# Four experts tile by tile, finished rows on another queue, and weight loads moved and cut into 4 KB packets, in a retention layer with a mixture of experts behind it

## The chip, the cores and the metric

The kernel runs on one core of a Trainium2 chip. The metric is device time in microseconds (us); lower is better. A profile shows one execution: which engine ran which instruction when, what each waited for, and what every DMA queue moved. Four sessions on chips were used. The three of the experiments are named by the number of the chip: 9, 8 and 7 (the first session gave no number). Executions are marked fast or slow by their time and the clock granted to TensorE; verdicts use fast ones.

How much can be believed: the kernel before, submitted again unchanged, came out at a ratio of 1.0195 (95% interval 1.0095 to 1.0296) to itself on the same chip. The changed kernel gave 0.9535 on chip 8 and 0.9727 on chip 7. So here a difference of under some 2% between two kernels is not resolved by time alone, whatever its interval says, and the traces have to carry such arguments.

## The reference

```
# attention: per batch (4) and head (8), 768 steps, head size 64
state = gamma[h] * state + outer(k[t], v[t])
y[t]  = scale * q[t] @ state
# experts: x = y as 3072 rows of 512
do_compute = x @ w_skip > 0
e_idx = argmax(x @ w_gate); gate = softmax(...)[e_idx]      # 8 experts
out = x;  out[row] = x[row] + gate * (relu(x[row] @ w1[e]) @ w2[e])   # where do_compute
```

The weights w1 and w2 are 8 x 2 MB each in fp32. They are turned into bf16 while they are loaded, on GpSimd's queue.

## The kernel before

Attention is done in 16 units (4 batches x 4 pairs of heads), of 7 to 9 us each. A unit transposes q and k (`tps`), makes the scores (`atps`) and the chunk sums (`kvps`, which need v), applies them (`yps`), transposes the result into rows (`xall`, `xlast`) and stores the rows. Rows of three finished batches are routed while the last batch runs. Then come expert tasks: gather up to 256 rows of an expert as two tiles of 128, layer 1 (`hps`), layer 2 (`yps2`; the profile shows it as `yps` too), add (`yo`), scatter. "Tile by tile" experts have two tasks: the first tile, made of rows of the first three batches, can start before the last batch is routed.

```
def load(i):                      # q, k, v of unit i, on SyncE's queue
    for w, src, tag, bufs in ((kw, k, "kw", 2), (qw, q, "qw", 2), (vn, v, "vn", 4)):
        w[i] = poolQ.tile([128, 2 * G, R * D], FP32, tag=tag, bufs=bufs, name=tag)
        ...
        nc.sync.dma_start(out=w[i][:, :, :], in_=rows)          # 384 KB in rows of 512 B

def load_w(e, which, pl):         # GpSimd's queue, fp32 -> bf16
    w1b[e] = pl.tile([128, NDB, F], BF16, tag=f"w1_{e}", bufs=1, name="w1b")
    return G_.dma_start(out=w1b[e][:, :, :], in_=moe_w1[e].rearrange("(p a) f -> p a f", p=128))
    # 16 KB read in one piece per partition
    ...

def t_x(i, a):                    # rows of unit i
    ...
    for g in range(G):
        (A_ if last and g == 1 else nc.sync).dma_start(out=rows[...], in_=src[...])

wunits = (1, 4, 7, 9, 11, 12, 13, 13, 14, 15)   # units at which a weight load is issued
for i in range(NU):
    scale_qk(i + 1)               # GpSimd
    for _ in range(wunits.count(i)):
        load_w(*wjobs.pop(0), poolW)
    load(i + 3)
    ...                           # the unit; the first tiles are gathered in unit 15
NSPLIT = 3
tasks = [(e, [0]) for e in range(NSPLIT)] + [(e, [1]) for e in range(NSPLIT)] + [(e, [0, 1]) for e in range(NSPLIT, E)]
for t, (e, sts) in enumerate(tasks):
    hT = layer1(e, sts)
    ...                           # at t == 0: route the last batch, then gather the second tiles
    put_out(...)                  # VectorE adds, GpSimd scatters
    ...                           # gather later experts; six late weight loads, one a task
```

Of the kernel before, what the change touches and what calls it, by code (L numbers as in the profile page):

```python
# [18 lines left out]
def kernel(  # L19
# [17 lines left out]
    nc = tc.nc  # L37
    PE, V_, A_, G_ = nc.tensor, nc.vector, nc.scalar, nc.gpsimd
# [3 lines left out]
    E = moe_w1.shape[0]  # L42
# [7 lines left out]
    NU = B * NP  # L50
# [4 lines left out]
    CAP = 256  # L55
    NST = CAP // 128
    NEARLY = 10
    NSPLIT = 3
    scale = 1.0 / math.sqrt(D)
    lng = [math.log(1.0 - 2.0 ** (-5.0 - h)) for h in range(H)]  # L60

# [2 lines left out]
    poolW = ctx.enter_context(tc.tile_pool(name="wpool", bufs=1))  # L64
# [72 lines left out]
    for r in range(R):  # L137
        for hi in range(2):
            m = maskc[64 * hi : 64 * hi + 64, r, :, :]
            G_.affine_select(  # L140
                out=m, in_=m, pattern=[[1, R], [R, 64]], base=-r, channel_multiplier=-R, compare_op=ALU.is_ge, fill=0.0,
# [77 lines left out]

    w1b, w2b = {}, {}  # L220

    def load_w(e, which, pl):
        if which == 0:
            w1b[e] = pl.tile([128, NDB, F], BF16, tag=f"w1_{e}", bufs=1, name="w1b")
            return G_.dma_start(out=w1b[e][:, :, :], in_=moe_w1[e].rearrange("(p a) f -> p a f", p=128))
        else:
            w2b[e] = pl.tile([128, NFB, DM], BF16, tag=f"w2_{e}", bufs=1, name="w2b")
            return G_.dma_start(out=w2b[e][:, :, :], in_=moe_w2[e].rearrange("(p a) d -> p a d", p=128))


    QT, KT, ATm, Y, xT, xall = {}, {}, {}, {}, {}, {}
# [90 lines left out]
    def t_x(i, a):  # L322

        b, p = divmod(i, NP)
        last = i == NU - 1
        if p % 2 == 0 and a == 0:
            xall[b] = pool.tile([128, NS, 256], FP32, tag="xall", bufs=2, name="xall")
        if last and a == 0:
            xall["last"] = pool.tile([128, NS, 128], FP32, tag="xT", bufs=4, name="xlast")
        ps = ptile()  # L330
        for j in range(NT):
            PE.transpose(out=ps[:, j * 128 : (j + 1) * 128], in_=xT[i][:, a * NT + j, :], identity=ident[:, :])  # L332
        dst = xall["last"][:, :, :] if last else xall[b][:, :, p % 2 * 128 : (p % 2 + 1) * 128]
        A_.copy(
            out=dst[:, a * NT : (a + 1) * NT, :], in_=ps[:, :].rearrange("p (j t) -> p j t", j=NT),
        )
        rows = out[b * S : (b + 1) * S, :]
        if a == 0 or i < NU - 2 and p % 2 == 0:
            return
        src = xall["last"][:, :, :] if last else xall[b][:, :, 0:128] if i == NU - 2 else xall[b][:, :, :]  # L340
        cs = slice((p - 1) * 128 if i < NU - 2 else p * 128, (p + 1) * 128)
        for g in range(G):
            (A_ if last and g == 1 else nc.sync).dma_start(
                out=rows[g * 128 * R : (g + 1) * 128 * R, cs].rearrange("(p r) d -> p r d", r=R),
                in_=src[:, g * R : (g + 1) * R, :],
            )
# [160 lines left out]
    def gather(e, s_, first=True):  # L507
        n = (B - 1) * S if first and s_ == 0 else N
        ga = G_.indirect_dma_start(  # L509
            out=xgt[e, s_][:, :], out_offset=None, in_=out[0:n, :],  # L510
            in_offset=bass.IndirectOffsetOnAxis(ap=si[s_][:, e : e + 1], axis=0), bounds_check=n - 1, oob_is_err=False,
        )
        if first:
            no_dep(ga, scatters)
            gathers.append(ga)
# [15 lines left out]

    ALLV, IDS, GTS = slice(0, NV), slice(0, 2), slice(2, NV)
    wjobs = [(e, w) for e in range(E) for w in range(2)]
    wunits = (1, 4, 7, 9, 11, 12, 13, 13, 14, 15)
    routed = oh = None
    for i in range(NU):
        scale_qk(i + 1)
        if i == 1:
            parts = more_constants()
        for _ in range(wunits.count(i)):  # L540
            load_w(*wjobs.pop(0), poolW)
        load(i + 3)
        b, p = divmod(i - 2, NP)
        for a in range(2):
            t_qk(i, kw, KT, "KT", 1, a)
            t_qk(i, qw, QT, "QT", 2, a)
        if i >= 6 and p == 0:
            L = gate_rows(range(NP))
            routed = route(L)
        if i >= 6 and p == 2:  # L550
            tp = table(b - 1, oh, ALLV)
        s_at(i, 0)
        if i >= 6 and p == 2:
            add_table(tp)
        if i >= 2:
            t_x(i - 2, 0)
            t_x(i - 2, 1)
        if i >= 1:
            s_inter(i - 1)
        if i >= 2 and p == 3:  # L560
            gate_logits(b, range(NP))
        if i >= 6 and p == 0:
            cp = places(b - 1, routed[1])
            put_places(b - 1, routed[1], cp)
            oh = one_hots(b - 1, 0, G_)
            count(routed[1])
        if i == NU - 1:
            tp = table(b - 1, oh, ALLV)
            pad_counts()
            add_table(tp)  # L570
        s_at(i, 1)
        s_kv(i)
        if i >= 1:
            s_av(i - 1, 0)
            s_av(i - 1, 1)
        if i == NU - 1:
            s_av(i - 1, 2)
            slot_values(0)
            for e in range(NSPLIT):
                gather(e, 0)  # L580
        s_at(i, 2)
        if 1 <= i < NU - 1:
            s_av(i - 1, 2)
        if 1 <= i <= 3:
            parts[i - 1]()
        if i in (4, 5, 8, 9, 12, 13):
            n = (4, 5, 8, 9, 12, 13).index(i)
            V_.memset(xgt[n // 2, n % 2][:, :], 0.0)
        if i >= 6 and p == 0:
            gate_weight(b - 1, *routed, G_)  # L590
            put_rhs(b - 1, routed[1], ALLV, G_)
# [19 lines left out]
    poolE = ctx.enter_context(tc.tile_pool(name="esb", bufs=2, reuse_waits="tile"))  # L611
    for e, s_ in [(e, s_) for e in range(NSPLIT, E - 2) for s_ in range(NST)]:
        xgt[e, s_] = poolE.tile([128, DM], FP32, tag=f"xg{e}_{s_}", bufs=1, name="xgl")
    for n, (e, s_) in enumerate([(0, 0), (1, 0), (2, 0), (0, 1)]):
        xgt[E - 2 + n // 2, n % 2] = xgt[e, s_]
    poolX = ctx.enter_context(tc.tile_pool(name="wlate", bufs=1, reuse_waits="tile"))
    late = [(e, w, poolX) for e, w in wjobs]
# [45 lines left out]
    def clear_rows(e, s_):  # L663
        V_.memset(xgt[e, s_][:, :], 0.0)  # L664

    tasks = [(e, [0]) for e in range(NSPLIT)] + [(e, [1]) for e in range(NSPLIT)] + [(e, [0, 1]) for e in range(NSPLIT, E)]
    NAHEAD = 3
    after = None
    for t, (e, sts) in enumerate(tasks):
        hT = layer1(e, sts)  # L670
        if t == 2:
            tp = table(B - 1, oh, GTS, 1)
            V_.tensor_tensor(T[:, 1:2, GTS, :], T[:, 1:2, GTS, :], tp[:, :, :, :], ALU.add)
            V_.tensor_tensor(gt[1][:, :], T[:, 1, 2, :], T[:, 1, 3, :], ALU.add)
            V_.tensor_tensor(gt[1][:, :], gt[1][:, :], T[:, 1, 4, :], ALU.add)
        if t == 0:
            cp = places(B - 1, ha)
            put_places(B - 1, ha, cp)
            oh = one_hots(B - 1, 1)
            put_rhs(B - 1, ha, IDS)  # L680
        if t + 1 < len(tasks):
            e1, sts1 = tasks[t + 1]
            if 0 < t <= NAHEAD:
                for s_ in sts1:
                    x_cast(e1, s_)
            x_tr(e1, sts1)
            if NAHEAD <= t < len(tasks) - 2:
                for s_ in tasks[t + 2][1]:
                    x_cast(tasks[t + 2][0], s_)
        yps = [layer2(e, sts[0], hT, 0, t % 2)] if len(sts) == 1 else None  # L690
        if t == 0:
            prev = poolS.tile([128, E], FP32, tag="prev", bufs=1, name="prev")
            V_.tensor_tensor(prev[:, :], T[:, 1, 0, :], T[:, 1, 1, :], ALU.add)
            tp = table(B - 1, oh, IDS, 1)
            V_.tensor_tensor(prev[:, :], prev[:, :], tp[:, 0, 0, :], ALU.add)
            V_.tensor_tensor(si[1][:, :], prev[:, :], tp[:, 0, 1, :], ALU.add)
        if t == 1:
            for s_ in range(NST):
                clear_rows(NSPLIT + 1, s_)
                clear_rows(NSPLIT + 2, s_)  # L700
            count(ha)
            gate_weight(B - 1, Ls, ha)
            put_rhs(B - 1, ha, GTS)
        if t == 0:
            for n in range(NSPLIT):
                gather(n, 1)
            after = gathers[-1]
            for s_ in range(NST):
                clear_rows(NSPLIT, s_)
        with tc.issue_after(after.ins):  # L710
            for n, s_ in enumerate(sts):
                put_out(e, s_, yps[n] if yps else layer2(e, s_, hT, n, n))
        after = scatters[-1]
        with tc.issue_after(after.ins):
            for e1 in ((NSPLIT,), (NSPLIT + 1, NSPLIT + 2), (NSPLIT + 3,), (NSPLIT + 4,))[t] if t < 4 else ():
                for s_ in range(NST):
                    gather(e1, s_)
            if late:
                load_w(*late.pop(0))
# [63 lines left out]
```

## Time and profile before

| | before |
|---|---|
| timed runs, median of 3 | 245.79 us (244.05 to 247.15) |
| profiled run (the record marks it slow) | 237.03 us, span 235.0 us |
| TensorE busy | 199.5 us, 85% |
| first layer 1 starts | 157.28 us |
| last TensorE work | 223.6 us |

The page counts an engine's busy time; where the end is set is read from the chain of waits. The list of DMA issues tells how long each kind of transfer takes from issue to landing (count, KB each, median us). Two lines of it matter later:

```profile
vn<-in_v_dram SPq DMA_DIRECT2D x16, 384.0 KB, 7.3
out_dram<-xlast SPq DMA_DIRECT2D x2, 128.0 KB, 3.3
```

A v load usually lands 7.3 us after its issue, and the rows of the last unit in 3.3 us. The other lines are in the prediction below.

### The profile page before, as it was taken

What the parts mean: (1) busy time and instruction counts of PE and PEld (TensorE: products, weight loads), DVE (VectorE), ACT (ScalarE), POOL (GpSimd) and SP (SyncE); (2) the same over time, 40 slices, a digit from 0 to 9 for tenths busy, and PEclk for the clock granted to TensorE, in tenths of its full rate; (3) what the DMA queues carried; (4) which work ended last, traced back from release to release, by engine and by line L of the source; (5) the groups of instructions that cost most, each with busy time, mean ns of one, the idle gap of its engine ahead of it and who ended that gap; (6) DMA issues with size and microseconds to landing.
All of it is one profiled execution on the core that took longest, in us unless ns stands there. A gap on an engine that the chain in (4) does not pass through costs nothing.

```text
span 235.0 us, 8033 instructions
## 1 busy us (share of the span) xinstructions
PE 199.5 (85%) x3362; PEld 165.9 (71%) x3362; DVE 128.6 (55%) x432; ACT 79.4 (34%) x191; POOL 111.9 (48%) x131
## 2 busy tenths in 40 slices
PE   7779998999999999977998804988789999999900
PEld 7669987979899789966797604776557878866600
DVE  3557757649965488646298601458844644253120
ACT  2333354445543643452551400233203234322400
POOL 5169525324996356972177600503777754331220
PEclk9889999999999999999999965999979999999995
DMA  3899999999829999999999998260499999982120
GB/s 93 240 267 262 219 264 264 211 283 314 248 70 192 326 270 290 276 207 218 293 253 217 219 226 281 66 197 9 150 173 275 241 243 235 236 228 91 56 81 4
DMA packets 51096, 48.71 MB, mean 207 GB/s; under 512 B 3717, under 2 KB 47493, under 8 KB 49009
## 3 DMA queue, kind: packets, MB, share of 16 engines
q0 software_dynamic: 4864, 22.97, 43.3%
q1 hardware_dynamic: 45920, 25.06, 37.2%
q8 instruction: 28, 0.46, 0.8%
q10 hardware_dynamic: 272, 0.13, 0.2%
q14 instruction: 12, 0.09, 0.1%
HBM read 56.64 MB, written 10.49 MB: 286 GB/s over the span
## 4 chain that ended last, share of the span: by engine, by line
PE 70%; DMA 12%; DVE 7%; issue 3%; SPq 2%; POOL 1%; ACT 0%; DVEq 0%
DMA vn<-in_v_dram 12%; PE hps L630 11%; PE yps L640 11%; PE atps L257 10%; PE yps L308 8%; PE tps L243 8%; PE yps L297 7%; PE tps L332 5%; PE kvps L278 5%; PE gps L354 2%; SPq L92 2%; PE xtp L528 2%; DVE Zb L290 1%; DVE xgl L664 1%; PE lps L369 1%
## 5 line engine op out<-in xcount | busy, mean ns | idle before, releaser
L262 DVE TENSOR_TENSOR ATm<-atps,maskc 128x256 f32<-128x256 f32 x96 | 36.0, 416 | 31.7 <-PE atps L257 31.0
L290 DVE TENSOR_TENSOR Zb<-kvps,Zb 64x64 f32<-64x64 f32 x128 | 28.4, 222 | 17.1 <-ACT Zb L288 13.5
L113 POOL TENSOR_TENSOR ks<-kw,tk 128x768 f32<-128x768 f32 (+1 forms) x18 | 24.3, 1351 | 25.4 <-DMA kw<-in_k_dram 11.1
L257 PE MATMUL atps<-QT,KT 64*64 64x128 f32 x768 | 34.6, 284 | 1.4 <-DVE ATm L262 1.2
L634 ACT ACTIVATE hT<-hps 128x512 bf16<-128x512 f32 x32 | 19.1, 597 | 46.5 <-PE hps L630 46.5
L113 POOL TENSOR_TENSOR qs<-qw,tq 128x768 f32<-128x768 f32 x15 | 22.4, 1496 | 23.8 <-DMA qw<-in_q_dram 15.4
L308 PE MATMUL yps<-ATm,vn 64*64 64x128 f32 x768 | 31.1, 278 | 2.2 <-issue 2.2
L630 PEld LDWEIGHTS <-w1b 128*128 128x128 bf16 x352 | 30.6, 144 | 2.5 <-issue 0.8
L630 PE MATMUL hps<-xgT,w1b 128*128 128x128 bf16 (+1 forms) x352 | 31.1, 246 | 0.7 <-DVE xgT L529 0.7
L640 PE MATMUL yps<-w2b,hT 128*128 128x512 bf16 x128 | 30.7, 391 | 0.0
L257 PEld LDWEIGHTS atps<-QT,KT 64*64 64x64 f32 x768 | 24.0, 136 | 8.1 <-ACT QT L244 3.6
L651 POOL DMA_INDIRECT out_dram<-yo,si x16 | 16.3, 1021 | 23.9 <-DVE yo L648 15.9
L308 PEld LDWEIGHTS yps<-ATm,vn 64*64 64x64 f32 x768 | 24.8, 137 | 3.0 <-issue 2.9
L278 PE MATMUL kvps<-vn,ks 64*64 64x64 f32 x640 | 16.1, 230 | 10.0 <-DMA vn<-in_v_dram 10.0
L509 POOL DMA_INDIRECT xg<-out_dram,si x10 | 10.4, 1039 | 27.6 <-DVE gt L488 15.5
L278 PEld LDWEIGHTS kvps<-vn,ks 64*64 64x64 f32 x640 | 15.4, 145 | 10.4 <-issue 10.2
L640 PEld LDWEIGHTS <-hT 128*128 128x128 bf16 x128 | 12.5, 101 | 13.5 <-issue 1.6
L288 ACT COPY Zb<-kvps 64x64 f32<-64x64 f32 x32 | 6.6, 206 | 43.4 <-PE kvps L278 43.0
L297 PE MATMUL yps<-QT,Zb 128*128 128x128 f32 x160 | 20.7, 276 | 0.5 <-DVE xT L317 0.5
L297 PEld LDWEIGHTS yps<-QT,Zb 128*128 128x128 f32 x160 | 19.1, 192 | 0.9 <-ACT xT L317 0.7
L463 POOL TENSOR_SCALAR oh<-iotab,posT 128x256 bf16<-128x256 bf16 x18 | 16.3, 916 | 6.3 <-DVE posT L426 6.3
L243 PE MATMUL tps<-ident,ks 128*128 128x128 f32 x96 | 17.2, 287 | 1.7 <-ACT xT L317 1.3
(127 smaller groups left out, 261.3 us busy)
## 6 DMA issues: line engine op xcount, KB each, us to landing
w1b<-in_moe_w_dram POOLq DMA_DIRECT2D x8, 1024.0 KB, 11.0
w2b<-in_moe_w_dram POOLq DMA_DIRECT2D x8, 1024.0 KB, 10.9
vn<-in_v_dram SPq DMA_DIRECT2D x16, 384.0 KB, 7.3
kw<-in_k_dram SPq DMA_DIRECT2D x15, 384.0 KB, 6.2
qw<-in_q_dram SPq DMA_DIRECT2D x15, 384.0 KB, 6.8
out_dram<-xall SPq DMA_DIRECT2D x21, 256.0 KB, 6.3
kw<-in_k_dram SPq DMA_DIRECT2D x6, 64.0 KB, 1.9
qw<-in_q_dram SPq DMA_DIRECT2D x6, 64.0 KB, 1.9
```

Source lines behind the costliest of these rows:

```text
L113: eng.tensor_tensor(scaled[tag][:, ns, :, :], raw[:, ns, :, :], sc, ALU.mult)
L243: PE.transpose(out=ps[:, j * 128 : (j + 1) * 128], in_=in_, identity=ident[:, :])
L257: PE.matmul(out=ps[h][cp, j * C : (j + 1) * C], lhsT=KT[i][hp, s_, cp], rhs=QT[i][hp, R * g : R * g + R, cp], start=True, stop=True,)
L262: V_.tensor_tensor(out=ATm[i, n][:, h, :, :], in0=ps[h][:, :].rearrange("p (c t) -> p c t", c=2), in1=maskc[:, :, :, :].rearrange("p c r t ...
L278: PE.matmul(out=ps[c][64 * h : 64 * h + 64, g * D : (g + 1) * D], lhsT=kw[i][cp, R * g + r, h, :], rhs=vn[i][cp, h * G + g, r * D : (r + 1 ...
L290: V_.tensor_tensor(z, kv, Zb[i % 2][c - 1][hp, hp], ALU.add)
L297: PE.matmul(out=Y[i, c][:, g, :], lhsT=Zb[i % 2][ch - 1][:, :], rhs=QT[i][:, R * g : R * g + R, 64 * c : 64 * c + 64], start=(ch <= 2), st ...
L308: PE.matmul(out=Y[i, c][64 * h : 64 * h + 64, g, :], lhsT=vn[i][cp, h * G + g, r * D : (r + 1) * D], rhs=ATm[i, s_ // 2][cp, h, s_ % 2, :] ...
L463: eng.tensor_scalar(o[:, :], iotab[:, 128 * s0 :], posT[:, j : j + 1], None, ALU.is_equal)
L630: PE.matmul(out=ps[:, f, :], lhsT=w1b[e][:, db, f0 + f :: NFB], rhs=xgT[e][:, db, 0:n], start=(db == 0), stop=(db == NDB - 1),)
L634: A_.activation(out=hT[:, f0 : f0 + nf, 0:n], in_=ps[:, :, :], func=AF.Relu, bias=0.0, scale=1.0)
L640: PE.matmul(out=ps[:, :], lhsT=hT[:, fb, n * 128 : (n + 1) * 128], rhs=w2b[e][:, fb, :], start=(fb == 0), stop=(fb == NFB - 1),)
```

## The change

The intent: keep the DMA queue free for the last q, k and v, let rows and weights share it in shorter turns, and give TensorE one more task that doesn't depend on the last batch. Moving cuts only renumber lines.

```
-    NSPLIT = 3
+    NSPLIT = 4
...
-            return G_.dma_start(out=w1b[e][:, :, :], in_=moe_w1[e]...)
+            return G_.dma_start(out=w1b[e][:, :, :], in_=moe_w1[e]..., max_dma_last_dim=most)     # w2 likewise
...
-            (A_ if last and g == 1 else nc.sync).dma_start(
+            (nc.sync if i >= NU - 2 and (g != 1 or not last) else A_).dma_start(
...
-    wunits = (1, 4, 7, 9, 11, 12, 13, 13, 14, 15)
+    wunits = (1, 4, 7, 10, 12, 13, 14, 14, 15)
-            load_w(*wjobs.pop(0), poolW)
+            load_w(*wjobs.pop(0), poolW, 4096 if i >= 12 else None)
...
             for e in range(NSPLIT):
                 gather(e, 0)
+            load_w(*wjobs.pop(0), poolW, 4096)
...
-        if i in (4, 5, 8, 9, 12, 13):          # clears a gather tile
+        if i in (3, 4, 5, 8, 9, 12, 13, 14):
...
-    for n, (e, s_) in enumerate([(0, 0), (1, 0), (2, 0), (0, 1)]):     # tiles used again by the last two experts
+    for n, (e, s_) in enumerate([(0, 0), (1, 0), (2, 0), (3, 0)]):
-    NAHEAD = 3
+    NAHEAD = 4
-                clear_rows(NSPLIT + 2, s_)
-            for e1 in ((NSPLIT,), (NSPLIT + 1, NSPLIT + 2), (NSPLIT + 3,), (NSPLIT + 4,))[t] if t < 4 else ():
+            for e1 in (NSPLIT + t,) if NSPLIT + t < E else ():
```

I call the parts P (packets of 4 KB), W (where weight loads stand), R (rows on ACT's queue) and N (four experts tile by tile).

More of the change, by code (lines that the diff above doesn't have):

```diff
@@ L220, with load_w @@
     w1b, w2b = {}, {}
-    def load_w(e, which, pl):
+    def load_w(e, which, pl, most=None):
         if which == 0:
             w1b[e] = pl.tile([128, NDB, F], BF16, tag=f"w1_{e}", bufs=1, name="w1b")
-            return G_.dma_start(out=w1b[e][:, :, :], in_=moe_w1[e].rearrange("(p a) f -> p a f", p=128))
+            return G_.dma_start(out=w1b[e][:, :, :], in_=moe_w1[e].rearrange("(p a) f -> p a f", p=128), max_dma_last_dim=most)
         else:
             w2b[e] = pl.tile([128, NFB, DM], BF16, tag=f"w2_{e}", bufs=1, name="w2b")
-            return G_.dma_start(out=w2b[e][:, :, :], in_=moe_w2[e].rearrange("(p a) d -> p a d", p=128))
+            return G_.dma_start(out=w2b[e][:, :, :], in_=moe_w2[e].rearrange("(p a) d -> p a d", p=128), max_dma_last_dim=most)
     QT, KT, ATm, Y, xT, xall = {}, {}, {}, {}, {}, {}
@@ L585 @@
             parts[i - 1]()
-        if i in (4, 5, 8, 9, 12, 13):
-            n = (4, 5, 8, 9, 12, 13).index(i)
+        if i in (3, 4, 5, 8, 9, 12, 13, 14):
+            n = (3, 4, 5, 8, 9, 12, 13, 14).index(i)
             V_.memset(xgt[n // 2, n % 2][:, :], 0.0)
```

## The prediction

> **What bounds the kernel now.** I read the page first, then the chain that ended last, in order of time.
>
> ```profile
> span 235.0 us, 8033 instructions
> PE 199.5 (85%) x3362; PEld 165.9 (71%) x3362; DVE 128.6 (55%) x432; ACT 79.4 (34%) x191; POOL 111.9 (48%) x131
> DMA  3899999999829999999999998260499999982120
> PE 70%; DMA 12%; DVE 7%; issue 3%; SPq 2%; POOL 1%; ACT 0%; DVEq 0%
> ```
>
> TensorE is the bound (85% busy, 70% of the chain), but the DMA engines are full for most of the first 145 us, and one DMA carries 12% of the chain. The chain in order of time shows which (start, us, what):
>
> ```profile
> 116.24 0.60 PE atps L257 x16
> 116.89 27.14 DMA vn<-in_v_dram
> 144.16 1.44 PE kvps L278 x38
> ```
>
> This is the last v load, for unit 15, the last (batch, head pair). It took 27.14 us where the median v load takes 7.3 us. What TensorE really lost is in the waits:
>
> ```profile
> PE kvps L278 <- DMA vn<-in_v_dram: 10.0, 1, 10.0
> ```
>
> The windows view puts a size to the hole and its neighbours (us, busy PE, PEld, DVE, ACT, POOL, then clock, DMA share, GB/s):
>
> ```profile
> 117.00:134.00 17.00, 15.93 (x343) 14.03 (x334) 13.97 (x48) 6.82 (x19) 12.78 (x18) 1.00 1.04 236
> 134.00:144.20 10.20, 0.17 (x12) 0.07 (x5) 1.01 (x5) 0.00 (x0) 0.00 (x0) 0.64 1.01 242
> 144.20:157.30 13.10, 11.88 (x209) 10.21 (x210) 5.64 (x22) 4.02 (x10) 3.10 (x3) 0.89 0.59 172
> 157.30:175.00 17.70, 14.40 (x155) 10.34 (x155) 12.17 (x47) 3.71 (x7) 10.04 (x10) 0.90 0.42 97
> ```
>
> From 134.0 to 144.2 nothing computes while the DMA engines are full. Why the v load is late is seen in the DMA queues of the window 125 to 140 us:
>
> ```profile
> DMA packets 883, 3.33 MB, mean 222 GB/s; under 512 B 65, under 2 KB 517, under 8 KB 517
> q0 software_dynamic: 410, 2.97, 94.6%
> q1 hardware_dynamic: 469, 0.31, 8.4%
> ```
>
> 883 - 517 = 366 packets are weights (8 KB written, 16 KB of fp32 read), 517 - 65 = 452 are rows of 0.5 to 1 KB. The two queues take turns about packet for packet, and a weight packet lasts 0.946 x 15 x 16 / 366 = 0.62 us. A row waits for a weight packet each time.
>
> The SyncE timeline adds a second cause: the issue of finished rows stood 12.95 us in front of the loads of unit 15.
>
> ```profile
> 101.47 12.95 SPq L343 DMA_DIRECT2D out_dram<-xall  x3
> 114.52 1.09 SPq L87 DMA_DIRECT2D kw<-in_k_dram  x1
> 116.89 1.53 SPq L87 DMA_DIRECT2D vn<-in_v_dram  x1
> ```
>
> **What the Trainium skill says.** "DMA: Bandwidth & Descriptors", Queues, rings and completion order: each DMA engine goes round its queues packet by packet. The trace agrees (452 rows against 366 weight packets). Same page, SWDGE vs HWDGE vs iDMA: a packet should preferably be at most 4096 B, since the engine changes queue only at its end; these are 16 KB on the read side. Same page, Issuing engines are not separate DMA queues: another issuer gives no bandwidth, only issue time. That is the use made of ACT here; no row of before tests it under load. "TensorE: Matmul & The Clock Gate", Part 1: after some microseconds idle the clock falls to half until work has run again. The trace agrees: clock 0.64 in the hole, 0.89 after it, and `kvps x38` takes 1.44 us against 0.63 in earlier units.
>
> **The change part by part.**
>
> *4 KB packets from unit 12 on.* An estimate from the 0.62 us above: a quarter, 0.155 us. A v load is 384 KB in rows of 512 B, 768 packets, 48 an engine. Behind 16 KB packets: 48 x (0.62 + 0.03) = 31 us while weights last (0.03 us a row from the window 50 to 60: 5415 packets took 112.7% of 10 x 16 us). They were gone at about 144, so 27.1 us is the same thing. Behind 4 KB packets: 48 x (0.155 + 0.03) = 8.9 us. Total bytes don't change.
>
> *Fewer weights before the last loads.* Ten weight loads stay ahead of the experts, six late ones after. Jobs move from units 9, 11, 12, 13, 13, 14, 15 to 10, 12, 13, 14, 14, 15 and one after the first gathers. Two loads (117.88 and 118.45) that stood beside the last v load now come a unit later, after the last q has been scaled (about 123).
>
> *Rows out on ACT.* 21 of the 27 issues move. SyncE no longer waits for ACT's copies in program order, so the loads of unit 15 go out when their buffers are free. vn has four buffers, so v of unit 15 needs the end of unit 12, about 110. Issued at 110 and 9 us long, it lands by about 119 to 122, and it is wanted at 134. The wait of 10.0 us goes whole. ACT pays three issues of about 0.6 us (the one issue it has today took 0.67), 1.8 us every second unit; between the xall copies and the next Zb copy ACT idles 1.87 us in its timeline. So it is hidden, just. I charge 0.5 us in all.
>
> *Clock after the hole.* kvps 1.44 -> 0.65 us is 0.8 us on the chain; the slower yps, tps and gps after it add some 0.4. I take 1.2 us.
>
> *Four experts tile by tile.* One expert at 7.43 us (layer 1 3.53, transposes 0.45, layer 2 3.45) becomes two tasks of 3.9 us (174.95 to 178.87): + 0.37 us. What the fourth is to do is fill holes: tasks 0 to 2 last from 157.28 to 174.95, 17.67 us, against 3 x 3.9 = 11.7. But the chain there names DVE:
>
> ```profile
> 165.49 2.11 DVE L664 MEMSET xgl<- 128x512 f32 x4
> 169.34 0.31 DVE L438 TENSOR_TENSOR rhsT<-ha,vals 128x144 bf16<-128x144 bf16 x1
> 170.71 0.60 DVE L519 CAST xb<-xg 128x512 bf16<-128x512 f32 x1
> 171.98 2.97 PE yps L640 x8
> ```
>
> The gather for second tiles landed at about 166, so the 6 us are DVE's order, not a lack of rows. The change takes two of the four memsets (2 x 0.53 = 1.05 us) off this chain and puts two into units 3 and 14. TensorE also waits less, so `yps x8` may not fall to 2.97 us (1.73 elsewhere); I count 0.9 of those 1.24 us. Sum: - 1.05 - 0.9 + 0.37 = - 1.6 us.
>
> *GpSimd.* Four times the descriptors on six loads. A load of 128 packets takes 0.57 us to issue today; I expect 0.6 to 1.5. In unit 14 two of them stand before the one-hots, which now wait 1.7 us for VectorE; up to 0.5 us may reach TensorE.
>
> Sum on the span: 235.0 - 10.0 - 1.2 - 1.6 + 0.5 + 0.5 = 223.2 us, a factor of 0.950. The timed runs are longer than the profiled one (245.79 against 237.03); nothing here says why. The factor gives 233.4, the difference of 11.8 gives 234.0. A slower execution leaves the DMA queue, if anything, more room to hurt, so I go a little below: 233.
>
> **The rivals.**
>
> 1. *The wait moves.* DMA share is 0.99 to 1.04 from 70 to 134 us, so the queue as a whole may be the bound, and a load a unit later may starve unit 13 or 14. For: GpSimd already waited 7.7 us for a q load around 110 to 116. Against: TensorE lost nothing by that, and a weight load less lies ahead of the last loads. It would give back 3 to 8 us: 236 to 241.
> 2. *ACT becomes the stall.* SyncE's row issues took up to 11 us when the queue was full. If ACT's do as well, its KT and QT copies are late and TensorE stops with them, seven times. For: the waits under load. Against: ACT has a queue of its own, with at most three row issues in it. Two microseconds each would be 14 us: no gain, 246.
> 3. *The experts starve.* Late weights start after the first scatter, which now stands behind one more gather (1.3 us). The last weights landed at about 212 and were wanted at 220; the experts here end some 1.6 us earlier. Margin about 5 us; I see no loss, at most 2 us.
> 4. *A larger gain.* If the holes of tasks 0 to 2 do close with more work, up to 4 us more go: 229.
>
> **Range and chances.** Centre 233. Rival 1 in part or a few blocked ACT issues give the upper end, 239; rival 4, and a longer hole in the timed runs than in the profile, the lower, 226. Two per cent faster means under 240.9: it fails only if most of the 10 us comes back. Faster 0.91, within 2% 0.08, slower 0.01.
>
> **What would show it.** In the profile after: the wait of kvps for vn under 1 us and no TensorE clock below 0.9 in that stretch; the last v load landing in under 12 us and q0 packets in the stretch of about 0.16 us; rows out on ACT's queue with issues of 0.5 to 0.8 us; `kvps` of unit 15 at 0.65 us; first layer 1 at about 146 instead of 157.28; the first four tasks about 1.5 us shorter than four of before; POOL's weight issues under 1.5 us. Wrong would be: a TensorE wait for another load over 3 us, ACT issues over 2 us with KT or QT late behind them, POOL blocked in a weight issue, or hps or yps waiting for w1b or w2b.

## The result, and the profile after

The changed kernel took 233.48 us (median of 4, 232.38 to 236.43) against 245.73 us of the kernel before (median of 4). The ratio is 0.9508, 95% interval 0.9428 to 0.9588. Ratios here are the mean time of one kernel's fast runs over that of the other's fast runs of the same rounds, so not quite the ratio of the medians quoted. Result correct.

The profiled execution of the changed kernel, 236.43 us, was a slow one. Its page:

```profile
span 234.7 us, 8080 instructions
PE 199.5 (85%) x3384; PEld 164.5 (70%) x3394; DVE 127.2 (54%) x432; ACT 79.0 (34%) x191; POOL 113.2 (48%) x131
DMA  3899999999269999999999999943799999930120
PE 75%; DVE 6%; issue 5%; DMA 4%; another core or an unknown queue 3%; SPq 2%; POOL 1%; ACT 0%; DVEq 0%
```

Set beside the span of 235.0 us before, nothing seems to be won. Two things are hidden in that. First, the profiled run of before, at 237.0 us, is 7 to 10 us shorter than its timed runs (244.1 to 247.2); the experiments show below that chips differ by such an amount. Second, the same windows as in the prediction show that the hole has gone from one place and that another has come:

```profile
117.00:134.00 17.00, 15.21 (x333) 13.58 (x325) 12.64 (x47) 6.82 (x19) 11.87 (x16) 1.00 1.09 210
134.00:144.20 10.20, 7.96 (x196) 6.66 (x195) 4.79 (x20) 1.76 (x5) 3.79 (x5) 1.00 1.08 237
144.20:157.30 13.10, 11.34 (x127) 8.50 (x122) 8.11 (x31) 4.51 (x10) 1.37 (x2) 1.00 0.87 199
157.30:175.00 17.70, 9.29 (x80) 6.26 (x82) 6.66 (x22) 1.30 (x3) 11.57 (x13) 0.71 0.63 153
```

TensorE works 7.96 us from 134.0 to 144.2 where it worked 0.17 us, at full clock. But from 157.3 to 175.0 it works 9.29 us against 14.40. TensorE's timeline shows both places (start, us, count, then the idle time before and what ended it):

```profile
134.60 0.52 PE L278 MATMUL kvps<-vn,ks 64*64 64x64 f32 x23
135.77 0.51 PE L278 MATMUL kvps<-vn,ks 64*64 64x64 f32 x15 [0.65 <-issue]
...
150.13 2.09 PE L631 MATMUL hps<-xgT,w1b 128*128 128x128 bf16 x32 [0.69 <-DVE xgT L529]
...
169.79 0.61 PE L528 MATMUL xtp<-identb,xb 128*128 128x128 bf16 x4 [7.91 <-DVE xb L519]
```

The chunk sums of unit 15 start at 134.60 without any wait for v. Layer 1 starts at 150.13, not 157.28. Then, in the third expert task, TensorE waits 7.91 us. VectorE's and ACT's timelines name what was waited for:

```profile
166.44 0.60 ACT L635 ACTIVATE hT<-hps 128x512 bf16<-128x512 f32 x1 [4.44 <-remote]
168.59 0.18 DVE L674 TENSOR_TENSOR T<-T,tabps 128x24 f32<-128x24 f32 x1 [6.41 <-remote]
```

Both wait for TensorE itself: the layer 1 matmuls of that task are recorded from 159.40 to 161.5 and those of the table (the routing values of the last batch, `tabps`) until 161.9, but their ends are signalled at 166.4 and 168.6. I call this the late signal. "remote" is only the reader's word for a semaphore whose release it could not place.

The parts of the change seen one by one: rows on ACT's queue take 1.90 us for three, and the v load of unit 15 goes out at 110.87 instead of 116.89 (ACT's and SyncE's timelines):

```profile
97.92 1.90 ACTq L343 DMA_DIRECT2D out_dram<-xall  x3
...
110.87 0.37 SPq L87 DMA_DIRECT2D vn<-in_v_dram  x1
```

The DMA queues between 125 and 130 us show weight packets alone, 414 in 102% of 5 x 16 us, so 0.20 us each on average:

```profile
q0 software_dynamic: 414, 0.84, 102.0%
```

And one thing that I had not foreseen, in the list of DMA issues: the last rows now land 8.8 us after their issue, 3.3 us before.

```profile
out_dram<-xlast SPq DMA_DIRECT2D x2, 128.0 KB, 8.8
```

### The profile page after: what moved, and what is told of

Its sections match the earlier page's. It is cut to its first block, busy times and chain, and to the rows that moved or that the text cites. A ratio compares the mean times of both kernels' runs of the same rounds, so it can differ in the third digit from the quotient of the medians.

```text
span 234.7 us, 8080 instructions
## 1 busy us (share of the span) xinstructions
PE 199.5 (85%) x3384; PEld 164.5 (70%) x3394; DVE 127.2 (54%) x432; ACT 79.0 (34%) x191; POOL 113.2 (48%) x131
## 4 chain that ended last, share of the span: by engine, by line
PE 75%; DVE 6%; issue 5%; DMA 4%; another core or an unknown queue 3%; SPq 2%; POOL 1%; ACT 0%; DVEq 0%
PE atps L257 12%; PE yps L641 11%; PE hps L631 10%; PE yps L308 10%; PE tps L243 9%; PE yps L297 8%; PE tps L332 5%; PE kvps L278 5%; DMA out_dram<-xlast 3%; PE gps L354 3%; SPq L92 2%; PE xtp L528 2%; DVE Zb L290 1%; PE lps L369 1%
## 5 line engine op out<-in xcount | busy, mean ns | idle before, releaser
L113 POOL TENSOR_TENSOR ks<-kw,tk 128x768 f32<-128x768 f32 (+1 forms) x18 | 24.3, 1351 | 24.6 <-PE kvps L278 16.2
L631 PEld LDWEIGHTS <-w1b 128*128 128x128 bf16 x384 | 31.6, 145 | 3.1 <-issue 1.3
L631 PE MATMUL hps<-xgT,w1b 128*128 128x128 bf16 (+1 forms) x384 | 31.9, 241 | 0.8 <-DVE xgT L529 0.7
L257 PEld LDWEIGHTS atps<-QT,KT 64*64 64x64 f32 x768 | 23.4, 132 | 11.5 <-issue 6.3
L308 PEld LDWEIGHTS yps<-ATm,vn 64*64 64x64 f32 x768 | 24.0, 133 | 2.6 <-issue 2.5
L509 POOL DMA_INDIRECT xg<-out_dram,si x12 | 12.3, 1024 | 20.8 <-DVE xb L519 12.2
L334 ACT COPY xall<-tps 128x384 f32<-128x384 f32 x30 | 13.0, 482 | 16.0 <-PE tps L332 16.0
L244 ACT COPY KT<-tps 128x384 f32<-128x384 f32 x32 | 15.6, 489 | 7.4 <-PE tps L243 7.0
```

Of the source, the lines that this page charges most:

```text
L113: eng.tensor_tensor(scaled[tag][:, ns, :, :], raw[:, ns, :, :], sc, ALU.mult)
L257: PE.matmul(out=ps[h][cp, j * C : (j + 1) * C], lhsT=KT[i][hp, s_, cp], rhs=QT[i][hp, R * g : R * g + R, cp], start=True, stop=True,)
L308: PE.matmul(out=Y[i, c][64 * h : 64 * h + 64, g, :], lhsT=vn[i][cp, h * G + g, r * D : (r + 1) * D], rhs=ATm[i, s_ // 2][cp, h, s_ % 2, :] ...
L631: PE.matmul(out=ps[:, f, :], lhsT=w1b[e][:, db, f0 + f :: NFB], rhs=xgT[e][:, db, 0:n], start=(db == 0), stop=(db == NDB - 1),)
```

## The experiments

Twelve runs of ten kernels in three sessions, all correct. Each row has the median of all its executions in the session, slow ones included (the ratios use fast ones alone); the last column is the start of the first layer 1 in the kernel's trace.

| session | kernel | median us | ratio to before (95%) | layer 1 starts |
|---|---|---|---|---|
| chip 9 | before | 234.57 (7 runs) | 1 | - |
| | before_again | 237.34 | 1.0195 (1.0095-1.0296) | 157.5 |
| | p_only | 231.44 | 0.9939 (0.9828-1.0049) | 150.6 |
| | w_only | 229.26 | none given | 146.5 |
| | r_only | 228.0 | 0.9785 (0.9661-0.991) | 153.5 |
| chip 8 | before | 247.18 (11 runs) | 1 | - |
| | after_again | 233.04 | 0.9535 (0.9446-0.9624) | 148.0 |
| | no_n | 234.46 | 0.9593 (0.9506-0.9681) | 148.3 |
| | n_only | 245.5 | 1.0074 (0.9981-1.0167) | 152.8 |
| | no_p | 237.09 | 0.9707 (0.9631-0.9782) | 150.6 |
| chip 7 | before | 244.89 (11 runs) | 1 | - |
| | before_third | 245.99 | none given | 150.9 |
| | after_third | 236.98 | 0.9727 (0.9651-0.9803) | 153.3 |
| | held_w | 234.53 | 0.9546 (0.9454-0.9639) | 149.9 |
| | all_p | 237.01 | 0.9709 (0.9627-0.9791) | 150.1 |

Where an interval was given here it was reported as "unclear" and not as a verdict; the first run's 0.9508 was reported as faster. Where no ratio was given I use the medians: w_only 229.26 / 234.57 = 0.977.

**before_again** (no edit).

> The kernel before, unchanged, to learn why its profiled run (237.0 us) was 9 us shorter than its timed runs (245.7). Theory A (the v wait varies from run to run): the new profile shows the wait of kvps for vn nearer 18 us than 10, and the rest as before. Theory B (the chip or the session differs): the profile and the timed runs agree with each other here, at one level, with the wait still about 10 us. Ratio 1.00 within 1% either way.

Theory B held on this chip: profile (237.20) and timed runs agree, and the wait is the same, to 0.01 us (TensorE's timeline):

```profile
144.37 1.44 PE L278 MATMUL kvps<-vn,ks 64*64 64x64 f32 x38 [10.04 <-DMA vn<-in_v_dram]
...
157.49 1.73 PE L630 MATMUL hps<-xgT,w1b 128*128 128x128 bf16 x26 [0.69 <-DVE xgT L529]
```

The ratio of 1.0195 was a miss: I had allowed 1%. It is the yardstick for all that follows.

**p_only**: part P alone.

```
-            load_w(*wjobs.pop(0), poolW)
+            load_w(*wjobs.pop(0), poolW, 4096 if i >= 12 else None)    # and most=None in load_w
```

> The kernel before with 4 KB packets alone for the weight loads from unit 12 on (five loads), the same loads in the same places. My theory (a row waits for a weight packet each time): the last v load lands in under 15 us, the wait of kvps is 0 to 3 us, and 8 to 11 us go, about 235. Rival (the DMA engines are full of bytes, so the order of packets does not matter): the load still lands with the last weights, the wait stays over 7 us and the time within 1%.

The last v load landed 6.7 us after its issue (115.9 to 122.6), not 27.1, and TensorE did not wait for it. A part of that is a head start: the packet records have the first weight packet 4.2 us after the issue of the v load here, and 2.7 to 3.5 us in the four traces with long packets. But once both queues are busy the rows also pass faster. The DMA queues in one microsecond, some 5 us after the issue of the v load, first in before_again (123.4 to 124.4), then in p_only (120.9 to 121.9; packets, MB, share of 16 engines):

```profile
q0 software_dynamic: 26, 0.21, 101.4%
q1 hardware_dynamic: 35, 0.02, 7.9%
```

```profile
q0 software_dynamic: 82, 0.17, 91.5%
q1 hardware_dynamic: 116, 0.06, 19.7%
```

In both the rows (q1) are 1.3 to 1.4 times as many as the weight packets (q0), so shorter weight packets let 3.3 times as many rows through in the same time. So the packets alone take the wait away, and the rival, that only bytes count, falls. Time: 0.9939, a smaller gain than I expected. A second wait stood behind the first (the waits between 130 and 160 us: engine, line, what for, us in total, times, longest):

```profile
DVE xb L519 <- DMA xg<-out_dram,si: 6.1, 1, 6.1
POOL xg L509 <- DMA out_dram<-xall: 5.7, 1, 5.7
PE xtp L528 <- DVE xb L519: 4.3, 2, 3.6
```

The gathers of the first tiles wait until the rows of the third batch are stored, and these rows are still queued on SyncE behind the v load and between the weights. TensorE loses 3.6 us of the gain there.

**w_only**: part W alone, 16 KB packets.

```
-    wunits = (1, 4, 7, 9, 11, 12, 13, 13, 14, 15)
+    wunits = (1, 4, 7, 10, 12, 13, 14, 14, 15)
+            load_w(*wjobs.pop(0), poolW)          # after the gathers of the first tiles
```

> The kernel before with only the weight loads placed as in the change (16 KB packets throughout). My theory: with two loads fewer in front of it the last v load lands by about 125, before it is wanted at 134, so the wait of 10 us goes: about 235. Rival (packets are what counts): two loads still overlap the v load, each row waits 0.65 us behind them, and the wait stays over 5 us: 240 or more.

The v load was issued at 109.9 and landed at 116.7, in 6.8 us, with long packets: the loads that would have stood beside it were not there yet. This trace is the cleanest one. Span 222.8 us against 235.2 of before_again on the same chip, and the first layer 1 at

```profile
146.48 2.13 PE L631 MATMUL hps<-xgT,w1b 128*128 128x128 bf16 x32 [0.69 <-DVE xgT L529]
```

which is 157.49 - 146.48 = 11.0 us earlier. The rival (packets are what counts) falls. The times agree less well: the median of 229.26 is 2.3% below before; the profiled execution, 224.64, was the fastest of the four.

**r_only**: part R alone.

```
-            (A_ if last and g == 1 else nc.sync).dma_start(
+            (nc.sync if i >= NU - 2 and (g != 1 or not last) else A_).dma_start(
```

> The kernel before with only the row stores on the queue of ACT. My theory: the last q, k, v go out some 7 us earlier, so that most of the v load passes before the weight loads of unit 13 begin: the wait falls to 0 to 5 us, 236 to 240. Rival 2 of the prediction (ACT blocked in its DMA issues): no gain or a loss, with ACT issues over 2 us and KT or QT copies late.

No wait for v; but the v load went out at 120.6, later than before, and landed in 6.4 us, almost before its weights (their first packet comes 5.3 us after its issue). So it is not "issued 7 us earlier" that helped in this trace: that detail of my theory is wrong for it. What differs in this trace is that no row store stood behind or before it on its queue and that the weights came later after it; which of the two helped is not shown.

Rival 2 of the prediction shows here, once. The three row issues at 116.08 took ACT 6.46 us instead of 1.9 (the single issues 0.5 to 0.9 us, the rest lies between them), and the copies behind them were late (ACT's timeline, then TensorE's):

```profile
116.08 6.46 ACTq L343 DMA_DIRECT2D out_dram<-xall  x3
122.59 0.86 ACT L359 COPY Gs<-gps 128x384 f32<-128x384 f32 x2 [6.15 <-issue]
```

```profile
123.21 0.52 PE L243 MATMUL tps<-ident,ks 128*128 128x128 f32 x3 [1.77 <-ACT Gs L359]
```

TensorE lost 1.77 us there and 1.01 us soon after, behind a copy on VectorE. What stretched the issues is not known. The profiled execution was a slow one, with its units late from the third on; the median, 228.0, is the lowest of the session, 2.8% under before.

**after_again** (no edit to the changed kernel).

> The changed kernel, unchanged, beside the kernel before on one chip. Its first profile showed a hole of 7.9 us in the third expert task, in which layer 1 that TensorE had begun at 159.4 ended only at 166.4. Theory A (an accident of that execution, like the waits named issue that every profile has in other places): the hole isn't there, the first layer 1 starts at 146 to 150 and the span is 223 to 228. Theory B (made by the change): it is there again at the same place, over 4 us. Ratio to before: on the evidence of the three parts (0.97 to 0.99 each) 0.96 to 0.97 and not 0.951, since before ran at 234.6 us in the last session and at 245.7 in the first.

0.9535, lower than I expected from the parts on chip 9, and near the first 0.9508. Theory A failed: the late signal came again in the third task, with a gap of 6.6 us on TensorE. So it isn't an accident of one execution.

**no_n**: the changed kernel without N.

> The changed kernel with three experts tile by tile as before (packets, load order and row queue of the change kept). The prediction: the fourth expert was worth 1.6 us, so this one is 1 to 2 us slower than the changed kernel. Rival (a hole that is DVE's order is not filled, and two short tasks cost 0.4 us more than a long one): equal or up to 1 us faster.

234.46 against 233.04: 0.6% or 1.4 us slower, where I had predicted 1.6. It has the sign and the size, but it is under the yardstick of 2%, so it is not shown.

**n_only**: N alone on the kernel before.

> The kernel before with four experts tile by tile and nothing else. The prediction: the wait of 10 us for vn stays, tasks 0 to 3 take 1.5 us less, the whole is 0.5 to 1% faster. Rival: within 0.5% of before.

1.0074 (0.9981 to 1.0167): no gain seen. The trace surprised in another way: TensorE's wait for v was 2.5 us, not 10. The late signal was there too (gap of 5.5 us), although this kernel has none of P, W and R.

**no_p**: the changed kernel with 16 KB packets.

> The changed kernel with 16 KB packets throughout. If any one of the three parts takes the v wait away, as the last runs suggest, the packets add nothing beside the other two: within 0.5% of the changed kernel, no wait of kvps for vn over 1 us. Rival (they protect other loads): over 1% slower, with a wait for q, k or v over 2 us. The rows of the last unit should land sooner after their issue than in the changed kernel (8.7 us there), if four times more turns are what held them, or later, if long packets are.

No wait for v, as expected, yet 237.09 against 233.04, 1.7% slower. Not resolved, by the yardstick. In its trace the first layer 1 starts 2.6 us later than in after_again; the gaps named issue in the last two units are longer (1.20, 2.01 and 0.94 us against 0.64). Its last rows landed after 8.3 us (8.1 in after_again), so the size of the packets is not what holds them.

**before_third** (the kernel before) and **after_third** (the changed kernel), on chip 7.

> The kernel before once more, to get its trace in the session of the others. On the chip of the first and third sessions, where its timed runs take 242 to 250 us, I expect the wait for vn (up to 10 us) and also the hole of 5 to 8 us in the third expert task that all five traces from that chip show and none of the five from the other: layer 1 of the third task signals its end over 3 us late, and ten matmul records are missing (3352 against 3362). If the session falls on the other chip, neither the hole nor the missing records, and a span of about 235.

> The changed kernel in the same session. On the chip of the first and third sessions: 233 us, ratio 0.95, the hole again. On the other chip, where it has not run: no hole, the first layer 1 at 146 to 150, a span of 222 to 226 and a ratio near 0.965. That would mean that the part of the gain that comes from the v wait is 10 to 13 us on both, and that the session only adds a hole to both kernels.

The expectations mean chip 8 by "the chip of the first and third sessions" (for the first that was a guess) and chip 9 by the other; the session fell on neither. On chip 7 the kernel before has the late signal: TensorE waits 7.6 us in the third task. It also has fewer matmul records than on chip 9 (page):

```profile
PE 202.1 (85%) x3352; PEld 168.3 (70%) x3362; DVE 129.9 (54%) x432; ACT 79.2 (33%) x191; POOL 112.1 (47%) x131
```

So the late signal goes with the chip or the session, or with how it is recorded there, and not with the change. The four traces of chip 9 and the first trace of before have 3362 records and no late signal; all those of chips 7 and 8, and the first trace of after, lack 10 records and have it. The first trace of before (235.0) therefore looks as if it came from a chip of the other kind than its timed runs (245.7). That is a reading of likeness; no record of that session says so.

The wait for v was 4.0 us here, and what followed it is the second wait again (waits between 120 and 180 us):

```profile
POOL xg L509 <- DMA out_dram<-xall: 12.9, 1, 12.9
PE kvps L278 <- DMA vn<-in_v_dram: 4.0, 1, 4.0
DVE xb L519 <- DMA xg<-out_dram,si: 3.6, 1, 3.6
```

The rows of the third batch, issued at 118.5, landed at 143.4, 24.9 us later; only then could the first tile be gathered (145.1). In the three traces of the changed kernel those gathers wait for VectorE's gate values and not for rows.

after_third gave 0.9727; I had expected 0.95. Its profiled execution (240.81) was the slowest of its six and that of before_third (240.61) the fastest of its own, so the two spans, 239.0 and 238.7, say nothing about the gain. In after_third TensorE lost over 7 us to gaps named issue in the attention units (0.97, 0.86, 1.92, 1.47, 1.74, 0.67).

**held_w**: the changed kernel with the tenth weight load after the gathers of the second tiles.

```
             for e in range(NSPLIT):
                 gather(e, 0)
-            load_w(*wjobs.pop(0), poolW, 4096)
...
+    held = wjobs.pop(0)
...
             for n in range(NSPLIT):
                 gather(n, 1)
             after = gathers[-1]
+            with tc.issue_after(after.ins):
+                load_w(*held, poolW)
```

> The changed kernel with the tenth weight load, w2 of the fifth expert, held back until after the gathers of the second tiles. My theory: that load is what makes the last rows land 8.7 us after their issue (3.3 in the kernel before) and the gathers of the second tiles start 7 to 8 us after the first layer 1 instead of 5. Held back, rows land in under 5 us and those gathers start at 5 to 6 us. In time 0 to 2 us (the waits after it are mostly VectorE's). Rival: the gathers are on the path and 2 to 4 us go. If w2 then comes late, TensorE waits for it at the fifth expert.

The mechanism is shown. The last rows land in 2.3 us and the gathers of the second tiles start at 155.07, 5.2 us after the first layer 1 (149.9), as soon as VectorE has the row numbers (DMA issues; GpSimd's timeline):

```profile
out_dram<-xlast SPq DMA_DIRECT2D x2, 128.0 KB, 2.3
```

```profile
155.07 1.00 POOL L509 DMA_INDIRECT xg<-out_dram,si  x1 [10.68 <-DVE si L697]
```

In the changed kernel it was 157.79 - 150.13 = 7.7 us. No wait for the held weights appeared. The median is 234.53 against 236.98 for after_third, 1.0% less; the ratios to before (0.9546 and 0.9727) differ by more, since half of held_w's runs count as slow, the profiled one too. It may be the best version, but the yardstick doesn't let me say so. The late signal stayed (gap of 6.2 us), so it isn't the gathers' timing that makes it.

**all_p**: the changed kernel with 4 KB packets for the first four loads too.

```
-            load_w(*wjobs.pop(0), poolW, 4096 if i >= 12 else None)
+            load_w(*wjobs.pop(0), poolW, 4096)
```

> The changed kernel with 4 KB packets for all weight loads of the attention stage, the first four too. Long packets cost no_p 4 us against the changed kernel although no load was waited for; if what they delay is TensorE's instruction fetch (the waits named issue just after a packet of the instruction queue), short packets everywhere take 0.5 to 2 us more off. Rival (the 4 us were something else): within 0.5% of the changed kernel.

237.01 against 236.98: the rival held. Short packets early do nothing, and the thought that long packets delay instruction fetches found no support here.

## Why the prediction was right or wrong

The forecast of 233.0 us (226 to 239) met 233.48. By its steps:

1. **The v wait (10.0 us) goes: right, but it is not a constant.** No trace with P, W or R has it. P, W and R each take it away alone, so their gains don't add, as the prediction assumed in giving the wait once. But the 10.0 is the size of two traces (10.03 and 10.04); two others of the kernels with that queue had 4.0 and 2.5. "A row waits for a weight packet each time" was a little too strong: the prediction's own lines have 452 rows in 15 x 16 us, so 0.53 us a row and not 0.65. How many rows pass before the weights come matters: in before, before_again and before_third the first weight packet starts 2.7, 3.0 and 3.5 us after the issue of the v load (packet records), and the load lands after 27.1, 25.8 and 21.3 us. It isn't the whole: in n_only it starts after 2.9 us, and TensorE goes on with v 21.7 us after the issue. There the fourth weight load was issued 17.7 us after the v load, against 14.7 to 16.2 us in the other three, so the weights paused: in the microsecond that begins 20.1 us after the v load 436 rows pass and the weight queue is busy 0.2% of the time; in before, 46 rows beside 98.1%. Whether this wait is why the kernel before spread over 241 to 252 us on chip 7 is not shown either.
2. **Clock after the hole (1.2 us): right where it can be read.** The clock was 1.00 in the three windows from 117 to 157.3 us. On chip 9 the sum of points 1 and 2, 11.2 us, came out as 11.0 (w_only against before_again, one fast execution each). The changed kernel itself was not run on chip 9. On the other chips its layer 1 began at 150.1, 148.0 and 153.3 against the 146 predicted: gaps named issue, 0.6 to 2 us each, took what is missing in part. One of 0.65 us stands inside `kvps` of unit 15, so that this step took 1.68 us from start to end (134.60 to 136.28) and not the 0.65 us forecast.
3. **4 KB packets, 0.155 us: too small by a little.** 102% of 5 x 16 us over 414 packets is 0.20 us on average where they ran alone; the median duration of a weight packet in the trace's DMA records is 0.173 us (0.624 for a 16 KB one). 8.9 us for a v load beside weights was never tested: in p_only, where weights came only in the last 2.5 us, it took 6.7.
4. **Rows on ACT: right for the changed kernel, though the charge of 0.5 us was not measured by itself.** In its three traces three issues together took 1.9 to 3.2 us. With long packets and early loads (r_only) they once took 6.46 us, which cost TensorE some 2.8 us. The use I named (SyncE no longer waits) held, with v out at 110.87. What I missed is a greater use: the stored rows feed the gathers, and in the kernel before they lie behind weights for up to 26 us. In p_only this second wait cost TensorE 3.6 us, a part of why P alone gives less.
5. **Four experts (1.6 us): unresolved.** 1.4 us by no_n, none by n_only. A part was put down to the wrong cause: the prediction counted 0.9 us here for a faster `yps` in the third task, but w_only, without N, already has it (1.89 us in the timeline, 3.19 in before_again), and its first four tasks take 20.0 us against 21.4. In the first trace of the changed kernel they take 27.7 us, 7.9 of it the late signal's hole. Rival 4, that more work fills the holes of tasks 0 to 2, did not show.
6. **GpSimd's descriptors: right on the issue time.** A load in 4 KB packets takes 0.75 to 0.83 us to issue, against 0.57 (0.6 to 1.5 expected). Whether the 0.5 us charged to TensorE came was not tested.
7. **Not foreseen:** the tenth load beside the last rows (8.8 us to land), shown by held_w, and the late signal of the third task.

Rival 1 (the wait moves) thus holds in small: the last rows took it. The page's chain does go through them (`out_dram<-xlast`, 3%), but it goes on to a VectorE memset that starts 5.2 us after the first layer 1 with and without them (155.30 in the changed kernel, 155.09 in held_w), so they cost next to nothing. Rival 2 (ACT held up by its issues) occurred in r_only, not in the changed kernel. Rival 3 did not occur.

That the number came so near has luck in it. The factor of 0.950 was worked out from a trace that has the v wait at 10 us and no late signal, and applied to timed runs of a chip that seems to be of the other kind. There I cannot show how the 12 us are made up: on chip 7 and 8 the profiled executions with the old queue were the fastest of theirs, and show 4.0 and 2.5 us of v wait, the rows' wait, and tasks that take 76.4 us from the first layer 1 to TensorE's last work against 71.7 to 74.2 in the three traces of the changed kernel.

**Open:** what delays the end of layer 1 in the third task by 3 to 8 us on chips 7 and 8 in both kernels. TensorE's records are incomplete in just these traces, so the recording itself may have a part in it; no run tells. The missing ten are not in the hole, though: all are of layer 2 (118 `yps` records of 128), one each in ten of its sixteen tiles, from the first task on. What the gaps named issue are is open as well.

## What to carry to other kernels

Where two queues take turns packet by packet, as here, the long packets set how fast the short ones pass: a load that is wanted soon must be out before the long ones are queued, or the long ones must be cut. Here one of the two was enough; what remains is to look for the next transfer that stood behind the same queue, here the stored rows that the gathers wait for. And before explaining 2%, run the unchanged kernel against itself.

## What the Trainium skill lacked or had wrong

- "DMA: Bandwidth & Descriptors", Queues, rings and completion order, says that an engine changes between queues after a packet of typically 9 to 17 descriptors. Here each 16 KB piece of a weight load is a packet of its own: 366 of them took turns with 452 row packets of 0.5 to 1 KB. The page gives no figure for what a short packet pays for it: 0.53 us a row (15 x 16 / 452), a 384 KB load landing in 27.1 us instead of 6.7.
- None of the pages read for this case tells what cutting into 4 KB packets costs (0.75 to 0.83 us of GpSimd's time an issue instead of 0.57), nor that a load with a cast keeps 16 KB packets unless told otherwise, as here.
- "DMA: Bandwidth & Descriptors", Issuing engines are not separate DMA queues, says that another issuer saves only the sequencer's time. No run here tests the bandwidth, but the order can be worth more than the issue time: in r_only, which moves only the rows, the rows land after 9.7 us (median; a slow execution) and the gathers no longer wait for them, where in p_only, on SyncE's queue, they held the gathers up for 5.7 us. (In w_only the rows stay on SyncE's queue and the gathers don't wait for them either, so it is one way of two.)
- None of the pages read for this case has chips that differ as these did: the same kernel at 234.6 us on chip 9 and 247.2 and 244.9 on chips 8 and 7, with layer 1 signalled 3 to 8 us late in the third task and 10 matmul records missing on the latter two.
